# A recurrent attention with a feed-forward layer: negations ahead of masks, loads and stores moved among the queues, the A·B stage cut in halves

## The chip, the cores and the metric

The kernel runs on one core of a Trainium2 chip. A core has a matrix engine (TensorE, PE in the profile, with PEld for its weight loads), VectorE (DVE), ScalarE (ACT), GpSimd (POOL) and SyncE (SP), which here only issues DMAs. Each engine takes its instructions in the order of the program and waits on semaphores for the others; a DMA that waits on SP's queue holds up every DMA behind it. The metric is the device time of one execution in microseconds (us).

## The reference

Batch 4, 8 heads, 768 tokens, head size 40: 32 independent heads. Each keeps a 40x40 state that every token changes; the outputs go through a two-layer feed-forward net (called MoE in the code, though it has one expert).

```python
for t in range(S):
    y[:, :, t] = einsum('bhd,bhde->bhe', rt, state)
    Sa = einsum('bhde,bhe->bhd', state, at)
    state_decay = state * wt[:, :, None, :] - einsum('bhd,bhe->bhde', Sa, bt)
    state = state_decay + einsum('bhd,bhe->bhde', vt, kt)
...
h = x @ w_in                       # x: 3072 x 320, w_in: 320 x 2048
g = where(h >= 1, h, where(h <= -1, 0, (h + 1)**2 / 4))
return g @ w_out                   # w_out: 2048 x 320
```

All is float32.

## The kernel before, in words

**Chunks.** The 768 tokens are cut in 24 chunks of 32. Within a chunk the recurrence is written as matrix products, which need running products of w along the tokens and, for each head and chunk, the inverse of a triangular 32x32 matrix. Six sets of four chunks share this preparation; sets 0 and 1 are prepared before the main loop, but for the inverse of set 1.

**Three background stages** prepare a set s while the chunks of earlier sets run. *rows* (`prelude`, lines 217 to 262) takes four parts of eight tokens each. A part loads tiles of w, a, k and b (line 225), forms running products P of w on DVE (L237 to L243), multiplies a with them on POOL (L245), forms reciprocals on DVE (L249, L252), multiplies k (L255) and b (L257) with them on POOL, and stores the four products from the tile `arena` to a DRAM scratch `scr` (L258, issued by POOL). `arena` holds one part at a time. The tile of `b` is that of `a` (tag "a"). *ab* (`ab_set`, from line 276) reads rows of `scr` back into `tiab`, transposes them (L287, DVE), multiplies them in 32 small matmuls (L298), copies the result from PSUM (L303, ACT) and stores it to `abd` (L306). *inv* (`invert`) reads `abd` and inverts by 62 steps on POOL (L326 and L332) into `ttd`.

**The chain.** `chain(c, hb)` runs chunk c for heads 0 to 15 (hb 0) or 16 to 31 (hb 1) in five steps, with matmuls at L468, L479, L497, L526 and L536. After the second, DVE multiplies with the mask (L486) and ACT negates (L490); both read one of two PSUM tiles, of four head pairs each, and write one tile `cg`. At the fourth step ACT and POOL round the outputs into `Y` (L516, L517). `turn` (L423, L426, L428) transposes token rows from the tiles `ti`, `scores` multiplies them (L438) and masks them (L447). `cg` and `ti` are loaded from `scr` and `ttd` by L398, L401, L409 and L274.

**The feed-forward net.** After every second chunk `relayout` copies 64 tokens of `Y` into a tile `X` by nine DMAs on SP (L552 to L562). `moe` is a generator: for each of 16 blocks of 128 hidden columns, eight matmuls (L607), the activation on ACT (L613, L614) and DVE (L620), a split into a rounded part and a rest (L594 on ACT, L595 on POOL), and later six matmuls into `po` (L581, L585). At a group's end ACT copies `po` (L588) and SP stores it (L590).

**What sets the order.** The order is written out by hand. The main loop calls `step` ten times a chunk; a step runs one step of the chain, then three times `feed`, which takes 1024 columns of the feed-forward net's matmuls, and `background`. `feed` starts five steps after the first relayout, and from there one group of 64 tokens takes 20 steps, as long as two chunks. `background(n)` runs each stage in proportion to the weights that its generator yields, spread over a window of steps:

```python
WINDOWS = dict(
    rows=[(0, 0), (20, 36), (38, 68), (68, 103), (107, 147)],
    ab=[(0, 0), (38, 53), (68, 89), (108, 129), (147, 169)],
    inv=[(16, 36), (53, 72), (90, 112), (129, 152), (170, 192)],
)
ROWS_W = (2, 1, 1.5, 3, 2, 13)
AB_W = (1, 6, 3, 8, 15)
```

Steps within ten count unequally (`SHARE`). From step 192 on no background is left. Until the first relayout PE has only the chain, and `weights` converts the two weight matrices beside it.

## Time and profile before

| | us |
|---|---|
| median of 3 runs | 977.39 (974.42 to 980.83) |
| profiled execution | 976.18 |
| its span | 974.4 |
| PE busy | 775.0 (80%) |
| DVE busy | 590.4 (61%) |
| ACT busy | 478.6 (49%) |
| POOL busy | 443.8 (46%) |
| mean granted clock of TensorE | 0.85 |

In the profile, "L490" is line 490 of the kernel. A row of the order of time gives the start, the duration, the engine and line, what is written and read, the shape and the count of merged instructions, and in brackets how long the engine was idle before, and what ended that. "SPq" is a DMA issue on SyncE's queue. Names as "cg<-p" are tiles: written, then read.

### The profile page before, as it was taken

To read this page: it belongs to the slowest core of one execution; us is meant where nothing else is said; L and a number is where in the kernel's file an instruction comes from. 1 tells how busy PE (TensorE), PEld (TensorE's weight loads), DVE (VectorE), ACT (ScalarE), POOL (GpSimd) and SP (SyncE) were. 2 spreads that over 40 slices of the span, in tenths; PEclk is the share of its full clock that TensorE was granted. 3 is DMA by queue.
4 is the path that set the end of the run, shared out by engine and by line. 5 is a ranking of instruction groups with operands and counts; after the bars stand their busy time and mean duration, and the time that the engine had idled before them with its cause. 6 is when DMAs were issued, how large, how long until landed. Compare 5 with 4: busy or idle time off the path is not lost.

```text
span 974.4 us, 35827 instructions
## 1 busy us (share of the span) xinstructions
PE 775.0 (80%) x14976; PEld 692.1 (71%) x14976; DVE 590.4 (61%) x1562; ACT 478.6 (49%) x1230; POOL 443.8 (46%) x673
## 2 busy tenths in 40 slices
PE   4523543447886988799879798989999999999995
PEld 3312532336776887688879687978898899999995
DVE  7782876574756583775654774776665556655321
ACT  5822444212543544454445454546565566656663
POOL 5200223686331599332588232697235962222332
PEclk9755555575997789797999796999999999999998
DMA  8799995565677755896735886856855545552010
GB/s 274 148 193 245 202 207 151 141 139 134 146 156 152 163 138 115 178 186 130 179 100 117 182 160 133 173 135 131 146 115 121 110 101 111 105 90 56 16 36 14
DMA packets 276866, 134.64 MB, mean 138 GB/s; under 512 B 194984, under 2 KB 266856, under 8 KB 276704
## 3 DMA queue, kind: packets, MB, share of 16 engines
q1 hardware_dynamic: 273504, 121.20, 57.9%
q0 software_dynamic: 3200, 11.14, 3.8%
q8 instruction: 118, 1.93, 0.9%
q14 instruction: 44, 0.36, 0.1%
HBM read 96.83 MB, written 33.82 MB: 134 GB/s over the span
## 4 chain that ended last, share of the span: by engine, by line
PE 34%; DMA 16%; POOL 16%; DVE 12%; issue 8%; SPq 8%; ACT 4%; POOLq 0%; ACTq 0%; DVEq 0%
PE ph L607 11%; PE po L581 6%; POOL lw L326 5%; POOL lw L332 4%; DMA ti<-scr 4%; PE po L585 3%; PE p L497 3%; POOL gl L595 3%; SPq L274 3%; PE p L468 3%; PE p L526 2%; DMA ld_a<-in_a_dram 2%; PE p L438 2%; PE p L479 2%; PE p L536 1%
## 5 line engine op out<-in xcount | busy, mean ns | idle before, releaser
L607 PE MATMUL ph<-X,w 120*128 120x256 f32 x1536 | 260.9, 307 | 51.6 <-DVE qt L620 44.3
L595 POOL TENSOR_TENSOR gl<-qt,gh 128x256 fp32r<-128x256 f32 x192 | 140.9, 734 | 280.0 <-ACT gh L594 264.6
L607 PEld LDWEIGHTS ph<-X,w 120*128 120x128 f32 x1536 | 219.8, 203 | 68.1 <-DVE qt L620 51.3
L620 DVE SCALAR_TENSOR_TENSOR qt<-qt,ph 128x256 f32<-128x256 f32 x192 | 79.9, 416 | 150.3 <-ACT qt L614 148.3
L581 PE MATMUL po<-wide,gh 128*128 128x320 f32 x768 | 163.7, 329 | 0.3 <-ACT gh L594 0.3
L594 ACT CAST gh<-qt 128x256 fp32r<-128x256 f32 x192 | 78.0, 406 | 167.6 <-DVE qt L620 166.7
L581 PEld LDWEIGHTS po<-wide,gh 128*128 128x128 f32 x768 | 124.6, 202 | 3.7 <-ACT gh L594 0.5
L613 ACT ACTIVATE qt<-ph,half_c 128x256 f32<-128x256 f32 x192 | 91.1, 474 | 53.4 <-POOL gl L595 39.7
L585 PE MATMUL po<-wide,gl 128*128 128x320 f32 x384 | 99.6, 338 | 17.6 <-POOL gl L595 17.6
L497 PE MATMUL p<-cg 128*64 128x72 f32 (+1 forms) x1536 | 74.8, 262 | 44.2 <-DVE cg L486 39.7
L497 PEld LDWEIGHTS p<-cg 128*64 128x64 f32 x1536 | 66.8, 166 | 54.3 <-ACT cg L490 45.0
L326 POOL TENSOR_TENSOR lw<-lw 128x31 f32<-128x31 f32 (+15 forms) x155 | 94.4, 609 | 18.0 <-DMA lw<-abd 9.3
L490 ACT ACTIVATE cg<-p 32x160 f32<-32x160 f32 x192 | 56.8, 296 | 87.9 <-DVE cg L486 61.0
L447 DVE TENSOR_TENSOR cg<-p,mask 32x256 f32<-32x256 f32 x192 | 80.6, 420 | 25.8 <-PE p L438 23.2
L332 POOL TENSOR_TENSOR lw<-lw 128x31 f32<-128x31 f32 (+15 forms) x155 | 84.1, 543 | 8.8
L504 DVE SCALAR_TENSOR_TENSOR cg<-p,pr 40x160 f32<-40x160 f32 x184 | 59.1, 321 | 41.1 <-PE p L497 39.2
L614 ACT ACTIVATE qt<-qt 128x256 f32<-128x256 f32 x192 | 80.2, 418 | 6.1
L585 PEld LDWEIGHTS po<-wide,gl 128*128 128x128 f32 x384 | 65.6, 197 | 23.9 <-POOL gl L595 21.5
L468 PE MATMUL p<-cg 128*64 128x72 f32 x1536 | 66.4, 243 | 16.7 <-DMA cg<-ttd 15.0
L486 DVE SCALAR_TENSOR_TENSOR cg<-p,mask 32x128 f32<-32x128 f32 x192 | 55.2, 288 | 36.2 <-PE p L479 30.7
L468 PEld LDWEIGHTS p<-cg 128*64 128x64 f32 x1536 | 58.7, 149 | 23.6 <-issue 19.0
L526 PE MATMUL p<-ident,cg 40*64 40x40 f32 x1472 | 57.1, 238 | 1.9 <-issue 1.9
(104 smaller groups left out, 1027.9 us busy)
## 6 DMA issues: line engine op xcount, KB each, us to landing
ti<-scr SPq DMA_DIRECT2D x96, 200.0 KB
ti<-scr SPq DMA_DIRECT2D x96, 168.0 KB
scr<-arena POOLq DMA_DIRECT2D x16, 640.0 KB, 5.4
cg<-scr SPq DMA_DIRECT2D x96, 80.0 KB
X<-Y SPq DMA_DIRECT2D x36, 160.0 KB
scr<-wide SPq DMA_DIRECT2D x8, 640.0 KB
tiab<-scr SPq DMA_DIRECT2D x32, 160.0 KB
scr<-in_r_dram SPq DMA_DIRECT2D x24, 160.0 KB
```

Of the source, the lines that this page charges most:

```text
L326: eng.tensor_mul(t3, W3[:, 0:n, j : j + 1].broadcast_to([128, n, m]), L3[:, j + 1 :, j].unsqueeze(1).broadcast_to([128, n, m]),)
L332: eng.tensor_sub(W3[:, 0:n, j + 1 :], W3[:, 0:n, j + 1 :], t3)
L447: nc.vector.tensor_tensor(out=cg[q, f::2, C_X : C_X + 64][:, 4 * i : 4 * i + 4].rearrange("p h (j x) -> p h j x", x=32), in0=ps[quarter(f, ...
L468: nc.tensor.matmul(psv[h // 8][64 * (1 - f) : 64 * (1 - f) + 64, h // 2 % 4, 0:72], lhsT=cg[:, h, C_T : C_T + 64], rhs=cg[:, h, C_R : C_R ...
L497: nc.tensor.matmul(psv[h // 8][64 * f : 64 * f + 64, h // 2 % 4, 0:n3], lhsT=cgw[:, h * CW + C_G : h * CW + C_G + 64], rhs=cg[:, h, C_R : ...
L581: nc.tensor.matmul(pos[i], lhsT=gh[:, ts_], rhs=w2[f // 8][:, j, f % 8, :], start=f == 0 and j == 0, stop=False)
L585: nc.tensor.matmul(pos[i], lhsT=gl[:, ts_], rhs=w2[f // 8][:, 0, f % 8, :], start=False, stop=f == NF - 1)
L595: nc.gpsimd.tensor_sub(gl, gt, gh.bitcast(F32))
L607: nc.tensor.matmul(ph, lhsT=w1[:, wi, fs], rhs=Xs[g][:, xi, :], start=i == 0, stop=i == 7)
L613: nc.scalar.activation(gt, ph, AF.Relu, bias=half_c, scale=0.5)
L614: nc.scalar.activation(gt, gt, AF.Square)
L620: nc.vector.scalar_tensor_tensor(out=gt, in0=gt, scalar=1.0, in1=ph, op0=ALU.min, op1=ALU.max)
```

## The change

- `ab_set` works on halves of eight head pairs: two transposes, 16 matmuls and one ACT copy of 128x128 each, in place of four, 32 and one of 128x256. The tile `ea` is half as large. Its weights `AB_W` are new. The early code that used the whole tile takes a second tag.
- `prelude` gives b a tile of its own. The first part's four loads go together. After that, the next part's a is asked for once the reciprocals are listed, w after the product with k, and k and b after the store.
- In `chain` the four negations on ACT are listed ahead of the four masks on DVE, both in the order half 0, half 1.
- ACT issues the output store.
- The two token loads (`load_ti`) and the relayout, but for the first and the last group, go one step later in the main loop.

```diff
--- before.py
+++ after.py
@@ -33,7 +33,7 @@
 SHARE = (3.1, 1.45, 0.93, 2.03, 0.6) * 2
 
 ROWS_W = (2, 1, 1.5, 3, 2, 13)
-AB_W = (1, 6, 3, 8, 15)
+AB_W = (1, 4, 8, 3, 6, 30)
 INV_W = 12
 
 TRAIL = 5
@@ -137,8 +137,6 @@
     turned = [
         [x[:, 0:2048].rearrange("p (n t) -> p n t", t=L) for x in xs] for xs in ((cgf[0], cgf[1]), (cgf[2], Yraw))
     ]
-
-    early_rows = {}
 
     def early_load(s):
         for x, n in zip(early_in[s], "wabk"):
@@ -190,9 +188,8 @@
     def early_ab(s, half):
 
         ps = psum()
-        if half == 0:
-            early_rows[s] = work.tile([128, 16, 2, 32], F32, tag="ea", name="ea").rearrange("p a b x -> p (a b x)")
-        ab = early_rows[s][:, 512 * half : 512 * half + 512]
+        tag = "ev" if half else "ea"
+        ab = work.tile([128, 8, 2, 32], F32, tag=tag, name=tag).rearrange("p a b x -> p (a b x)")
         for c in (2 * half, 2 * half + 1):
             for h in range(NH):
                 p, f = h // 2, h % 2
@@ -225,7 +222,7 @@
             nc.sync.dma_start(t, srcs[n][:, 4 * s : 4 * s + 4, 8 * part : 8 * part + 8, :])
             return t
 
-        wl, al, kl = load("w", 0, "w"), load("a", 0, "a"), load("k", 0, "k")
+        wl, al, kl, bl = (load(n, 0, n) for n in "wakb")
         pad_scr(s)
         yield 10
         for part in range(4):
@@ -244,21 +241,25 @@
             yield ROWS_W[0]
             nc.gpsimd.tensor_mul(at[:, 1:], al[:, 1:], P[:, :7])
             yield ROWS_W[1]
-            bl = load("b", part, "a")
             rec = work.tile([128, 8, D], F32, tag="ld_rec", name="rec")
             nc.vector.reciprocal(rec[:, 7], P[:, 7])
             yield 0.6
             for t in range(7, 0, -1):
                 nc.vector.tensor_mul(rec[:, t - 1], rec[:, t], wl[:, t])
                 yield 0.4
+            more = part < 3
+            if more:
+                al = load("a", part + 1, "a")
             yield ROWS_W[2]
             nc.gpsimd.tensor_mul(kt, kl, rec)
+            if more:
+                wl = load("w", part + 1, "w")
             yield ROWS_W[3]
             nc.gpsimd.tensor_mul(bt, bl, rec)
             nc.gpsimd.dma_start(scr[s][0 : NH * 128, 80:240].rearrange("(p t) x -> p t x", t=L)[:, ts_, :], R)
             yield ROWS_W[4]
-            if part < 3:
-                wl, al, kl = load("w", part + 1, "w"), load("a", part + 1, "a"), load("k", part + 1, "k")
+            if more:
+                kl, bl = load("k", part + 1, "k"), load("b", part + 1, "b")
             yield ROWS_W[5]
 
     def load_rows(dst, c, off, n, h0=0, nh=NH):
@@ -279,34 +280,38 @@
             reclaim(9)
             pad_rows(tiab, 48)
         load_rows(tiab, 4 * s, O_A, 80)
-        yield AB_W[4]
+        yield AB_W[5]
+        tv = tiab.rearrange("p h (j x) -> p h j x", x=40)[:, :, :, 0:32]
         for c in range(4 * s, 4 * s + 4):
-            ea = work.tile([128, 16, 2, 32], F32, tag="ea", name="ea")
-            tv = tiab.rearrange("p h (j x) -> p h j x", x=40)[:, :, :, 0:32]
-            for i in range(4):
-                nc.vector.transpose(ea[:, 4 * i : 4 * i + 4], tv[:, 4 * i : 4 * i + 4])
-                yield AB_W[0]
-            if c < 4 * s + 3:
-                load_rows(tiab, c + 1, O_A, 80)
-            yield AB_W[1]
-            ps = psum()
-            for p in range(16):
-                for f in range(2):
-                    rows = slice(64 * f, 64 * f + D)
-                    q = 2 * f + p % 2
-                    sl = p // 2
-                    nc.tensor.matmul(
-                        ps[32 * q : 32 * q + 32, 32 * sl : 32 * sl + 32],
-                        lhsT=ea[rows, p, 0, :], rhs=ea[rows, p, 1, :], start=True, stop=True,
-                    )
-            ab = work.tile([128, 8, 32], F32, tag="ab", name="ab")
-            nc.scalar.copy(ab, ps[:, 0:256].rearrange("p (s x) -> p s x", x=32))
-            yield AB_W[2]
+            for half in range(2):
+                if half:
+                    yield AB_W[2]
+                ea = work.tile([128, 8, 2, 32], F32, tag="ea", name="ea")
+                for i in range(2):
+                    nc.vector.transpose(ea[:, 4 * i : 4 * i + 4], tv[:, 8 * half + 4 * i : 8 * half + 4 * i + 4])
+                    yield AB_W[0]
+                if half and c < 4 * s + 3:
+                    load_rows(tiab, c + 1, O_A, 80)
+                yield AB_W[1]
+                if half == 0:
+                    ab = work.tile([128, 8, 32], F32, tag="ab", name="ab")
+                ps = psum()[:, 0:128]
+                for p in range(8):
+                    for f in range(2):
+                        rows = slice(64 * f, 64 * f + D)
+                        q = 2 * f + p % 2
+                        sl = p // 2
+                        nc.tensor.matmul(
+                            ps[32 * q : 32 * q + 32, 32 * sl : 32 * sl + 32],
+                            lhsT=ea[rows, p, 0, :], rhs=ea[rows, p, 1, :], start=True, stop=True,
+                        )
+                nc.scalar.copy(ab[:, 4 * half : 4 * half + 4], ps.rearrange("p (s x) -> p s x", x=32))
+            yield AB_W[3]
             for q in range(4):
                 nc.sync.dma_start(
                     abd[c // 4][q // 2, c % 4, q % 2 :: 2].rearrange("h t i -> t h i"), ab[32 * q : 32 * q + 32]
                 )
-            yield AB_W[3]
+            yield AB_W[4]
 
     def invert(s):
 
@@ -348,7 +353,7 @@
             done[key] = s
             yield 0
 
-    done, size, spent = dict(rows=1, ab=1), dict(rows=10 + 4 * (6.2 + sum(ROWS_W)), ab=AB_W[4] + 4 * (4 * AB_W[0] + sum(AB_W[1:4])), inv=INV_W + 67), {}
+    done, size, spent = dict(rows=1, ab=1), dict(rows=10 + 4 * (6.2 + sum(ROWS_W)), ab=AB_W[5] + 4 * (4 * AB_W[0] + 2 * AB_W[1] + sum(AB_W[2:5])), inv=INV_W + 67), {}
     back = {k: staged(*a) for k, a in dict(
         rows=("rows", None, prelude), ab=("ab", "rows", ab_set), inv=("inv", "ab", invert)).items()}
 
@@ -482,12 +487,13 @@
                 )
         for i in range(2):
             for f in range(2):
-                q = uq[f]
+                nc.scalar.mul(cg[uq[f], f::2, C_S : C_S + D][:, halves[i]], psv[i][quarter(f, i), :, 32:72], -1.0)
+        for i in range(2):
+            for f in range(2):
                 nc.vector.scalar_tensor_tensor(
-                    out=cg[q, f::2, C_R : C_R + 32][:, halves[i]], in0=psv[i][quarter(f, i), :, 0:32], scalar=-1.0,
+                    out=cg[uq[f], f::2, C_R : C_R + 32][:, halves[i]], in0=psv[i][quarter(f, i), :, 0:32], scalar=-1.0,
                     in1=mask[quarter(f, i)].unsqueeze(1).broadcast_to([32, 4, 32]), op0=ALU.mult, op1=ALU.mult,
                 )
-                nc.scalar.mul(cg[q, f::2, C_S : C_S + D][:, halves[1 - i]], psv[1 - i][quarter(f, 1 - i), :, 32:72], -1.0)
         yield
         psv = psum_2()
         n3 = 32 if last else 72
@@ -587,7 +593,7 @@
                     ob = mp.tile([128, 320], F32, tag="ob", name="ob", bufs=2)
                     nc.scalar.copy(ob, pos[i])
                     m = 128 // nt
-                    nc.sync.dma_start(ov[m * i : m * i + m, t0 : t0 + nt, :], ob)
+                    nc.scalar.dma_start(ov[m * i : m * i + m, t0 : t0 + nt, :], ob)
                 yield 320
 
         def split(g, f, gt, gh, gl):
@@ -844,6 +850,14 @@
             background(now[0] + (k + 1) / 3)
         now[0] += 1
 
+    def relayout_due(c):
+        g = c // 2 - 1
+        if c % 2 == 0 and g >= 0:
+            reclaim(5 + g % 2)
+            Xs[g] = relayout(g)
+            if idle[0]:
+                owed[0], idle[0] = -TRAIL * 3072, False
+
     for c in range(NC + 1):
         nxt = c + 1 < NC
         if c < NC:
@@ -851,18 +865,19 @@
         if nxt:
             load_cg(c + 1, 0)
         step(c, 0)
+        if 0 < c < NC - 1:
+            load_ti(c + 1, 1)
         if 0 < c < NC:
             scores(c, 1)
         step(c - 1, 1)
-        for g, (t0, nt) in enumerate(groups):
-            if t0 + nt == 32 * c:
-                reclaim(5 + g % 2)
-                Xs[g] = relayout(g)
-                if idle[0]:
-                    owed[0], idle[0] = -TRAIL * 3072, False
+        moved = idle[0] or c == NC
+        if moved:
+            relayout_due(c)
         if nxt:
             turn(c + 1, 0, 0)
         step(c, 0)
+        if not moved:
+            relayout_due(c)
         if nxt:
             turn(c + 1, 0, 1)
         step(c - 1, 1)
@@ -871,12 +886,12 @@
         step(c, 0)
         if nxt:
             turn(c + 1, 0, 2)
-            if c + 2 < NC:
-                load_ti(c + 2, 0)
         gens[c, 1] = chain(c, 1)
         if nxt:
             load_cg(c + 1, 1)
         step(c, 1)
+        if c + 2 < NC:
+            load_ti(c + 2, 0)
         if nxt:
             scores(c + 1, 0)
         step(c, 0)
@@ -889,8 +904,6 @@
         step(c, 1)
         if nxt:
             turn(c + 1, 1, 2)
-            if c + 2 < NC:
-                load_ti(c + 2, 1)
     for _ in mgen:
         pass
 
```

## The prediction

> **What bounds the kernel now.** I read the page first (shares, the clock row, the chain of waits), then the sums by stretch, then who waited for whom, and last the order of time around the longest waits. The page:
>
> ```profile
> span 974.4 us, 35827 instructions
> PEclk9755555575997789797999796999999999999998
> PE 34%; DMA 16%; POOL 16%; DVE 12%; issue 8%; SPq 8%; ACT 4%; POOLq 0%; ACTq 0%; DVEq 0%
> ```
>
> The profiled execution took 976.18 us, 1.8 more than its span; the median of the runs shown, 977.39, is 1.2 above that. TensorE (PE) holds a third of the chain of waits; DMA, GpSimd (POOL), VectorE (DVE) and SyncE's queue hold half. The sums by stretch show where; I cut them where the chain of heads 0 to 15 begins chunks 2, 4, 9, 13, 19 and 23 (a chunk is ten steps; chunks 9 to 12 are left out, and the last row is a short piece that I use below). Columns: stretch, its length, busy time of each engine, granted clock, DMA share, GB/s.
>
> ```profile
> 161.60:261.30 99.70, 59.26 (x1046) 53.03 (x1045) 63.72 (x170) 31.27 (x82) 63.40 (x98) 0.70 0.56 130
> 261.30:459.70 198.40, 173.18 (x3315) 153.36 (x3314) 124.33 (x369) 88.09 (x237) 94.37 (x141) 0.84 0.74 155
> 606.10:787.20 181.10, 173.52 (x3617) 155.47 (x3616) 115.79 (x305) 102.25 (x272) 114.78 (x184) 0.98 0.62 128
> 787.20:897.20 110.00, 110.00 (x2241) 99.93 (x2240) 67.57 (x180) 68.68 (x183) 34.12 (x53) 1.00 0.48 98
> 444.70:449.80 5.10, 5.10 (x107) 4.18 (x107) 0.01 (x1) 1.86 (x6) 0.73 (x1) 0.50 0.49 120
> ```
>
> From 787.2, with no background work left, four chunks take 110.0 us, 2.75 a step, and PE is busy throughout: nothing here touches that. From 261.3 to 459.7 five chunks take 198.4, 3.97 a step, 61 more than at 2.75; PE idles 25 of it, and most of the rest is a clock of 0.84. So what is to be won lies between 161.6 and the start of chunk 13, where the row products (rows) and the A·B matrices (ab) are made beside the chain. Who waited there (us in total, times, longest):
>
> ```profile
> ACT cg L490 <- DVE cg L486: 61.0, 20, 11.0
> DVE arena L239 <- DMA ld_a<-in_a_dram: 24.9, 5, 12.1
> POOL arena L257 <- DMA ld_b<-in_b_dram: 18.4, 7, 6.9
> DVE ea L287 <- DMA tiab<-scr: 18.4, 6, 6.0
> SPq L274 <- DVE pr L428: 63.1, 16, 10.4
> SPq L590 <- ACT ob L588: 41.8, 4, 27.2
> PE ph L607 <- DMA X<-Y: 6.5, 7, 2.2
> ```
>
> DVE is in order: while it waits for a load, the chain's masks (L486) and the MoE's L620 stand behind it, then ScalarE (ACT) behind L486, then PE behind L620.
>
> **Rows' loads.** The load of `a` for the next part used to need the tile that `b` had, so it could leave only after L257, the last product. Now it needs L245 only; `w` needs the reciprocals. Four waits hold 24.4 of the 24.9 us. But L239 writes the arena, which POOL's store L258 must have read: that wait comes next. The rows of the four, and the four stores before them:
>
> ```profile
> 188.35 0.96 POOL L258 DMA_DIRECT2D scr<-arena  x1 [0.30 <-POOL arena L257]
> 196.77 0.20 DVE L239 TENSOR_TENSOR arena<-ld_a,arena 128x40 f32<-128x40 f32 x1 [5.30 <-DMA ld_a<-in_a_dram]
> 236.01 0.93 POOL L258 DMA_DIRECT2D scr<-arena  x1 [0.30 <-POOL arena L257]
> 242.26 0.20 DVE L239 TENSOR_TENSOR arena<-ld_a,arena 128x40 f32<-128x40 f32 x1 [12.06 <-DMA ld_a<-in_a_dram]
> 409.94 0.93 POOL L258 DMA_DIRECT2D scr<-arena  x1 [0.30 <-POOL arena L257]
> 419.80 0.20 DVE L239 TENSOR_TENSOR arena<-ld_a,arena 128x40 f32<-128x40 f32 x1 [1.89 <-DMA ld_a<-in_a_dram]
> 435.30 0.93 POOL L258 DMA_DIRECT2D scr<-arena  x1 [0.30 <-POOL arena L257]
> 449.80 0.20 DVE L239 TENSOR_TENSOR arena<-ld_a,arena 128x40 f32<-128x40 f32 x1 [5.13 <-DMA ld_a<-in_a_dram]
> DMA to landing us min/median/max: 4.6/5.4/7.1
> ```
>
> With the median 5.4 the stores land at 193.8, 241.4, 415.3 and 440.7. DVE can start that much earlier: 3.0, 0.9, 1.9 (all of its wait) and 5.1 (all), 10.9 us together. PE does not get all of it: ahead of 449.80 it was busy 5.10 of 5.10. I take two thirds, **-7**; ends 0 and -11.
>
> `b` now has a tile of its own and is asked for with `k`, a part earlier than it is used, so the 18.4 us of L257 go, most of them in two waits:
>
> ```profile
> 315.53 0.87 POOL L257 TENSOR_TENSOR arena<-ld_b,rec 128x320 f32<-128x320 f32 x1 [6.15 <-DMA ld_b<-in_b_dram]
> 468.36 0.86 POOL L257 TENSOR_TENSOR arena<-ld_b,rec 128x320 f32<-128x320 f32 x1 [6.89 <-DMA ld_b<-in_b_dram]
> 471.26 0.90 PE L585 MATMUL po<-wide,gl 128*128 128x320 f32 x2 [2.29 <-POOL gl L595]
> ```
>
> After the second, PE lost 2.29 us on the MoE's gl queued behind it on POOL, a third of the 6.89. A third of 18.4 would be 6; the small waits cost nothing that I see, so **-4**; ends 0 and -6. The fourth load at a set's start goes last of the four and delays no first operand: 0; ends 0 and +1.
>
> **SyncE's queue.** The 24 output stores leave SP for ACT, and with them waits of 41.8 us for the copy, of which most lie after 897, where little is queued behind:
>
> ```profile
> SPq L590 <- ACT ob L588: 32.4, 2, 27.2
> ```
>
> The token loads go one step later, behind the six loads of the cg tile and no longer ahead of them; the relayout goes behind the third step's row loads. All arrive in time: token rows keep six steps (16.5 us at 2.75). The relayout's nine issues:
>
> ```profile
> 876.08 2.38 SPq L552 DMA_DIRECT2D X<-Y  x3
> 878.50 2.96 SPq L558 DMA_DIRECT2D X<-Y  x4
> 881.50 1.46 SPq L562 DMA_DIRECT2D X<-Y  x2
> 885.80 0.64 PE L607 MATMUL ph<-X,w 120*128 120x256 f32 x4
> ```
>
> They take 6.9 us on SP, and the MoE's first use is 9.7 us after the first. SP stood idle ahead of 876.08, waiting for POOL to round Y, so where no background runs a step's delay in the list moves nothing: 0; ends 0 and +2.75 for each of nine groups, +25. What SP's freedom is worth shows at one place of before, where a tiab load stood behind such a relayout:
>
> ```profile
> 278.91 1.06 DVE L287 STREAM_TRANSPOSE ea<-tiab 128x256 f32<-128x256 f32 x3
> 284.87 2.01 SPq L562 DMA_DIRECT2D X<-Y  x2
> 286.99 2.01 SPq L274 DMA_DIRECT2D tiab<-scr  x4
> 293.09 1.42 DVE L287 STREAM_TRANSPOSE ea<-tiab 128x256 f32<-128x256 f32 x4 [6.00 <-DMA tiab<-scr]
> 297.46 0.80 PE L607 MATMUL ph<-X,w 120*128 120x256 f32 x2 [4.37 <-DVE qt L620]
> ```
>
> DVE waited 6.00 and PE lost 4.37 after it. One such loss is what I credit SP with: **-4**; ends 0 and -10. Storing from ACT costs ACT an issue of its own, 24 x about 0.6 (a DMA issue above takes 0.5 to 0.8) = 14; ACT was busy 68.68 of 110.00 at the tightest, so **+1**; ends 0 and +14. The Trainium skill, page "DMA: Bandwidth & Descriptors", section "Issuing engines are not separate DMA queues", says that issuing from a second engine saves only the issuing time; by that rule the move gives the 14 us of issue to SP and no faster transfer.
>
> **The ab stage.** It is cut in halves of eight head pairs: transposes and matmuls stay in number, ACT's 16 copies become 32 half as wide (+16 x some 0.3, hidden as above). The weights matter more. Before, a set weighed 15 + 4 x 21 = 99, and from a tiab load to its transposes lay 6 + 3 + 8 = 17; now 30 + 4 x 29 = 146 and 4 + 3 + 6 = 13. Over windows of 15, 21, 21 and 22 steps that was 2.6, 3.6, 3.6 and 3.8 steps; it becomes 1.3, 1.9, 1.9 and 2.0: at 3.97 a step (3.02 in the last, 181.1 over 60 steps) 5.3, 7.4, 7.4 and 6.0 us. The load itself took 293.09 - 286.99 = 6.1 from its first issue. If SP is 2 us late (it was 7.0 late above; the new places lie mostly clear of the relayout and of the cg loads) the three such loads of a set wait 2.8, 0.7, 0.7 and 2.1 each, 19 us in all against 18.4 now. The planner's shares are uneven, down to one step, so I add 6 us of DVE waiting, at the 4.37 of 6.00 seen: **+4**; ends -6 and +35. The abd stores before the next copy lose time alike; inside these ends.
>
> **Negations first.** ACT's L490 shares each PSUM half with DVE's L486. Before, ACT began in the other half and then waited for DVE (61.0 us). Now ACT goes first and no longer stands behind a stalled DVE; instead each mask follows its negation.
>
> ```profile
> 862.94 1.29 DVE L486 SCALAR_TENSOR_TENSOR cg<-p,mask 32x128 f32<-32x128 f32 x4 [0.60 <-PE p L479]
> 863.00 1.23 ACT L490 ACTIVATE cg<-p 32x160 f32<-32x160 f32 x4 [0.58 <-PE p L479]
> 867.04 1.22 PE L497 MATMUL p<-cg 128*64 128x72 f32 x32
> ```
>
> Side by side they took 1.3 us; in file, 1.23 + 0.32. The next matmuls come 2.8 us after, so the 0.3 is covered by the other chain's step; uncovered it would be 48 x 0.3 = 15. In a stall, ACT saves its two late negations, 0.6 x 20 = 12 at most. Net **-2**; ends -12 and +15. The Trainium skill, page "PSUM — Partial Sum Buffer", section "Terms", has it that two engines may not touch one bank and quadrant at once, reads included; by that rule the masks must follow in file at every stage, which speaks against this order and would cost the 15 if nothing covered it.
>
> **The sum.** -7 - 4 - 4 + 1 + 4 - 2 = -12. Idling also lowers the clock: in the 5.10 us quoted at 0.50, PE was busy and did half the work, 2.6 us lost. I credit two such stretches, **-5**; ends 0 and -20. So 976.2 - 17 = 959; on the median, **960 us**.
>
> **The rivals.** *Waits replaced (no change).* Behind `a` stands the store's landing, behind `b` POOL's own inversion, behind SP's waits its issues, and the clock stays: only a's first 3.0 and half of what I credit `b`, SP and ACT with (5) remain, 8 less the 4 and 1 that ab and ACT's issues cost: 974, range 967 to 983. For it: two of the four waits end within 3.0 us of the landing. Chance 0.27.
> *The tiab loads become the bound (slower).* If SP stays as late as at 286.99, 7.0 us, each load needs 13.1, and the twelve wait 7.8, 5.7, 5.7 and 7.1 each: 79 us, 60 more than now; at 4.37 of 6.00 that is +44, for the +4 in the sum: 1000. With the other gains kept, it makes the kernel slower than before from a lateness of about 4.4 us, and by 1% from 5.5. Against it: the relayout and token loads, which made SP late, have moved. Chance 0.16.
> *The clock comes back (faster still).* In 261.3 to 459.7 PE was busy 173.2 at 0.84, 28 us of clock; in 161.6 to 261.3, 59.3 at 0.70, 18. If PE's stalls fall short enough, half of that 46 returns: 960 + 5 - 23 = 942. [...] Chance 0.12.
>
> **How the numbers follow.** The forecast has 0.45 (950 to 969). This kernel's runs tell 1% apart, 9.8 us: under 967.6 is faster, over 987.2 slower. Faster: 0.43 of the forecast, 0.12 of the clock, 0.02 of the replaced waits: 0.57; slower 0.16; within 1% 0.27. The range 940 to 983 leaves out most of the slower rival, 0.15, and 0.05 below.
>
> **What would show it.** Right: no wait of L239 on ld_a over 2 us but for landings of the arena's store; none of L257 on ld_b; ACT no longer waiting for L486; the clock above 0.84 from 261 to 460. Wrong: DVE's waits on tiab well over 18.4 us, PE's on X<-Y over 6.5, or DVE's masks waiting for ACT for tens of us with PE idle behind them; or the steps after the background's end longer than 2.75.

## The result, and the profile after

The changed kernel takes **1019.67 us** (1016.38 to 1022.89), the kernel before beside it 975.9: a ratio of **1.0439, 95% interval 1.0384 to 1.0494**. The forecast of 960 us and its range of 940 to 983 were wrong, and so was the sign. Of a few kernels below, one execution was over 1.5% longer than the fastest; the ratios leave such executions out, the medians do not.

The page of the changed kernel: span, clock by slices, shares of the chain of waits, and one of the DMA queues.

```profile
span 1019.6 us, 35949 instructions
PEclk9655555577776798886999887979798999999998
PE 37%; DMA 15%; POOL 13%; DVE 13%; issue 8%; SPq 7%; ACT 4%; DVEq 0%; POOLq 0%; ACTq 0%
q10 hardware_dynamic: 3120, 3.93, 1.2%
```

The shares hardly differ from before: the page alone doesn't say where 45 us went. q10 is new: the 24 output stores, 3.93 MB together, that ACT issues. The mean clock fell from 0.85 to 0.824.

The sums by stretch say where. These are cut at the beginnings of the same chunks as the rows before (2, 4, 9, then 13, 19, 23).

```profile
172.90:273.60 100.70, 65.16 (x1045) 57.74 (x1045) 65.02 (x170) 31.70 (x82) 63.33 (x98) 0.66 0.59 139
273.60:485.60 212.00, 179.05 (x3313) 157.94 (x3312) 125.40 (x366) 90.10 (x245) 93.36 (x140) 0.81 0.65 141
634.10:829.60 195.50, 185.70 (x3617) 166.10 (x3616) 118.33 (x314) 103.98 (x278) 116.17 (x185) 0.91 0.57 120
829.60:941.50 111.90, 110.59 (x2243) 100.02 (x2242) 66.45 (x176) 69.25 (x182) 34.20 (x53) 1.00 0.44 96
```

Up to chunk 2 the changed kernel loses 11.3 us (172.9 against 161.6), in the next two chunks 1.0 (100.7 against 99.7), in chunks 4 to 8 **13.6** (212.0 against 198.4, clock 0.81 against 0.84), in 9 to 12 2.1 (148.5, 485.6 to 634.1, against 146.4, 459.7 to 606.1), in 13 to 18 **14.4** (195.5 against 181.1, clock 0.91 against 0.98), in the four chunks without background 1.9, and in the tail 0.9. That sums to 45.2, the difference of the spans. Three places hold nearly all: the start, and two stretches where *rows* and *ab* run.

Who waited there (waits of the changed kernel: us in total, times, longest):

```profile
DVE cg L493 <- ACT cg L490: 52.6, 30, 4.2
DVE ea L291 <- DMA tiab<-scr: 50.8, 11, 9.8
ACT ab L308 <- DMA abd<-ab: 23.5, 5, 9.0
DVE ev L431 <- DMA abd<-ev: 14.4, 1, 14.4
DVE arena L236 <- DMA ld_a<-in_a_dram: 11.1, 1, 11.1
```

L493 is the mask, which was L486; L291 the transposes of ab, which were L287. The waits for the rows' loads went as forecast: none on `ld_b` is left, and one of five on `ld_a`. What came in their place is larger: the transposes wait 50.8 us for `tiab` in place of 18.4, the copies of ab 23.5 for the stores of the copy before, and the masks 52.6 for ACT, in the place of ACT's 61.0 for the masks. The fourth line is a wait that the prediction does not have at all.

The waits of SP's queue in the changed kernel (L222 is `load`, L275 `load_rows`, L311 the stores of ab, L403 and L406 the loads of cg):

```profile
SPq L311 <- DMA out_dram<-ob: 25.1, 5, 7.5
SPq L275 <- DMA out_dram<-ob: 23.4, 3, 10.0
SPq L222 <- DMA out_dram<-ob: 11.2, 2, 8.2
SPq L406 <- DMA out_dram<-ob: 7.2, 2, 3.6
SPq L403 <- DMA out_dram<-ob: 6.8, 2, 3.4
```

73.7 us in these five rows: SP, which no longer issues the output stores, waits for them. None of the waiting DMAs reads or writes `out` or `ob`. One of them, in order of time (SP, then ACT from the same stretch), and below it three pieces of the chain of waits at the same place (start, duration, what):

```profile
692.19 2.23 SPq L275 DMA_DIRECT2D tiab<-scr  x3
...
698.36 0.52 ACTq L596 DMA_DIRECT2D out_dram<-ob  x1
...
699.38 0.52 ACTq L596 DMA_DIRECT2D out_dram<-ob  x1
...
704.41 0.30 SPq L275 DMA_DIRECT2D tiab<-scr  x1
```

```profile
693.08 4.08 DMA tiab<-scr
698.36 6.03 DMA out_dram<-ob
704.41 4.05 DMA tiab<-scr
```

Three of a `tiab` load's four DMAs go out from 692.19. The fourth leaves at 704.41, ten microseconds after the third: it stood for the store that ACT issued only at 698.36, and then for that store's landing, 6.03 us later. The trace gives the semaphore that each DMA signals. SP's use eight, ACT's 24 stores the same eight, and POOL's eight others. The store of 698.36 and the fourth load signal the same one, number 108, and the fourth load's instruction waits on it before it goes. So the reading is: a DMA of SP that takes a semaphore whose last user was a store of ACT waits until that store has landed; the store itself waits for `po`, at the group's end; so SP is held by the end of the feed-forward group. The Trainium skill, page "DMA: Bandwidth & Descriptors", section "Why a DMA increments its semaphore by 16 and not by 1", says that a wait can pass too early where two DMAs in flight share one semaphore, which would be a reason for this order; the row above agrees in that the later DMA did not leave before the earlier one had landed, 6.03 us after its issue at 698.36.

### The profile page after: what moved, and what is told of

The parts are those of the page before. It is cut to its first block, busy times and chain, and to the rows that moved or that the text cites. A ratio compares the mean times of both kernels' runs of the same rounds, so it can differ in the third digit from the quotient of the medians.

```text
span 1019.6 us, 35949 instructions
## 1 busy us (share of the span) xinstructions
PE 800.5 (79%) x14976; PEld 712.8 (70%) x14976; DVE 594.1 (58%) x1562; ACT 483.3 (47%) x1246; POOL 443.2 (43%) x673
## 3 DMA queue, kind: packets, MB, share of 16 engines
q10 hardware_dynamic: 3120, 3.93, 1.2%
## 4 chain that ended last, share of the span: by engine, by line
PE 37%; DMA 15%; POOL 13%; DVE 13%; issue 8%; SPq 7%; ACT 4%; DVEq 0%; POOLq 0%; ACTq 0%
PE ph L613 12%; PE po L587 6%; POOL lw L331 4%; POOL lw L337 4%; PE po L591 4%; DMA tiab<-scr 3%; PE p L532 3%; PE p L503 3%; PE p L473 2%; POOL gl L601 2%; PE p L443 2%; DVE arena L240 2%; PE p L484 2%; PE p L542 2%; SPq L275 2%
## 5 line engine op out<-in xcount | busy, mean ns | idle before, releaser
L613 PE MATMUL ph<-X,w 120*128 120x256 f32 x1536 | 272.8, 315 | 46.0 <-DVE qt L626 41.5
L613 PEld LDWEIGHTS ph<-X,w 120*128 120x128 f32 x1536 | 228.3, 210 | 64.4 <-DVE qt L626 49.9
L587 PE MATMUL po<-wide,gh 128*128 128x320 f32 x768 | 167.1, 334 | 0.4 <-ACT gh L600 0.4
L587 PEld LDWEIGHTS po<-wide,gh 128*128 128x128 f32 x768 | 127.4, 206 | 3.8 <-ACT gh L600 0.7
L503 PE MATMUL p<-cg 128*64 128x72 f32 (+1 forms) x1536 | 71.5, 254 | 37.0 <-DVE cg L493 37.0
L452 DVE TENSOR_TENSOR cg<-p,mask 32x256 f32<-32x256 f32 x192 | 80.6, 420 | 27.9 <-PE p L443 25.3
L503 PEld LDWEIGHTS p<-cg 128*64 128x64 f32 x1536 | 63.8, 160 | 47.1 <-DVE cg L493 37.8
L493 DVE SCALAR_TENSOR_TENSOR cg<-p,mask 32x128 f32<-32x128 f32 x192 | 55.3, 288 | 56.2 <-ACT cg L490 52.6
L473 PEld LDWEIGHTS p<-cg 128*64 128x64 f32 x1536 | 58.9, 149 | 23.5 <-issue 14.8
L478 ACT COPY x<-p 128x288 f32<-128x288 f32 x96 | 36.6, 398 | 53.3 <-PE p L473 50.0
```

Of the source, the lines that this page charges most:

```text
L452: nc.vector.tensor_tensor(out=cg[q, f::2, C_X : C_X + 64][:, 4 * i : 4 * i + 4].rearrange("p h (j x) -> p h j x", x=32), in0=ps[quarter(f, ...
L473: nc.tensor.matmul(psv[h // 8][64 * (1 - f) : 64 * (1 - f) + 64, h // 2 % 4, 0:72], lhsT=cg[:, h, C_T : C_T + 64], rhs=cg[:, h, C_R : C_R ...
L503: nc.tensor.matmul(psv[h // 8][64 * f : 64 * f + 64, h // 2 % 4, 0:n3], lhsT=cgw[:, h * CW + C_G : h * CW + C_G + 64], rhs=cg[:, h, C_R : ...
L587: nc.tensor.matmul(pos[i], lhsT=gh[:, ts_], rhs=w2[f // 8][:, j, f % 8, :], start=f == 0 and j == 0, stop=False)
L613: nc.tensor.matmul(ph, lhsT=w1[:, wi, fs], rhs=Xs[g][:, xi, :], start=i == 0, stop=i == 7)
```

## The experiments

Times are medians, ratios are to the kernel before on the same chip, with 95% intervals. "After" is the changed kernel.

### Undoing one part of the change

**The store back on SP** (sp_store).

```diff
-                    nc.scalar.dma_start(ov[m * i : m * i + m, t0 : t0 + nt, :], ob)
+                    nc.sync.dma_start(ov[m * i : m * i + m, t0 : t0 + nt, :], ob)
```

> The changed kernel, with the 24 output stores issued by SyncE again. Theory A (a semaphore shared across queues): in the changed kernel 74 us of SyncE's waits are put down to DMA out_dram<-ob (25.1, 23.4, 11.2, 7.2 and 6.8), because a load or store on SyncE that takes the semaphore last used by a store of ScalarE's must wait until that store was issued, at a group's end, and has landed. Then those waits go, the four tiab loads no longer take 12.5 us to issue as at 692.2, and the time falls from 1019.7 by 10 to 20, to 1000 to 1010. Theory B (the shorter gap between a tiab load and its transposes is what costs): the stores are innocent, and the time stays within 3 us of 1019.7.

Measured: 1011.57 us, ratio 1.0341 (1.0254 to 1.0429); after had 1.0439 (1.0384 to 1.0494), and the intervals overlap. SP's waits for the landings are gone, except at the program's end, but SP now waits itself, since the store stands in its list right behind the copy:

```profile
SPq L596 <- ACT gh L600: 56.7, 9, 9.8
SPq L596 <- ACT ob L594: 32.4, 2, 27.2
```

In before, the second of them was 41.8, and the first less than half (SP's queue in before):

```profile
SPq L590 <- ACT gh L594: 24.6, 6, 9.1
```

So in the changed kernel SP stands for the stores on either queue, and undoing the move alone did not show what it is worth.

**The early code's second half in another tile** (early_x0). The early code makes two halves for each of two sets. Their tile `ev` carries the same tag as the tile of `turn` (L431), so `turn` for chunk 0 waits for the early halves' stores to land. Here the second half uses `x0`, a tile of another stage.

```diff
-        tag = "ev" if half else "ea"
-        ab = work.tile([128, 8, 2, 32], F32, tag=tag, name=tag).rearrange("p a b x -> p (a b x)")
+        if half:
+            ab = work.tile([128, 8, 72], F32, tag="x0", name="x0").rearrange("p a x -> p (a x)")[:, 0:512]
+        else:
+            ab = work.tile([128, 8, 2, 32], F32, tag="ea", name="ea").rearrange("p a b x -> p (a b x)")
```

> The changed kernel, with the second half of each early A-B matrix in the tile x0, which is first used later, in place of ev. In the changed kernel VectorE waits 14.4 us at 53 to 68 us for the store of that half before it may transpose token rows into ev, and chunk 0 begins 11.9 us later than before (91.5 against 79.6). If that wait is the cause, it goes and the time falls by 9 to 12, to 1008 to 1011. If the next wait (the inverse of set 0, the scr stores on SyncE) comes at the same moment, it falls by under 3.

Measured: 1006.94, ratio 1.0332 (1.0289 to 1.0375). Chunk 0 begins at 79.4 in place of 91.5, as in before (79.6). The first line is of the changed kernel, in the order of time:

```profile
68.04 0.71 DVE L431 STREAM_TRANSPOSE ev<-ti 128x512 f32<-128x512 f32 x1 [14.44 <-DMA abd<-ev]
```

and in early_x0 the same transpose follows L430 with no wait:

```profile
53.11 0.71 DVE L433 STREAM_TRANSPOSE ev<-ti 128x512 f32<-128x512 f32 x1
```

DVE's 14.4 us at the start are paid by the kernel nearly in full: 12.1 us of it.

**Wider spacing of ab** (ab_gaps). After, with weights by which a `tiab` load has 13 + 3 + 4 = 20 of 135 to its transposes, near before's 17 of 99, in place of 13 of 146.

```diff
-AB_W = (1, 4, 8, 3, 6, 30)
+AB_W = (1, 4, 2, 3, 13, 15)
```

> The changed kernel, with the weights of the ab stage set so that a tiab load has 20 of 135 units (15%) before its transposes, near the 17 of 99 of before, in place of 13 of 146 (9%). Theory B: VectorE's waits on tiab fall from 50.8 us (11 times) to 18 to 25, and the time by 12 to 22, to 998 to 1008. Theory A: the loads are late because SyncE is held, the waits stay above 35, and the time falls by under 5.

Measured: 1013.18, ratio 1.0394 (1.0341 to 1.0446), within the interval of after. The wait went, the time did not:

```profile
DVE ea L291 <- DMA tiab<-scr: 25.0, 6, 9.9
```

26 us less of DVE waiting, and some 4 of the kernel (0.0045 of 976), which the intervals do not tell from none. A theory that put the loss on the spacing alone falls here.

**All three together** (three_undone): the edits of sp_store, early_x0 and ab_gaps in one kernel.

```diff
-AB_W = (1, 4, 8, 3, 6, 30)
+AB_W = (1, 4, 2, 3, 13, 15)
...
-        tag = "ev" if half else "ea"
...
-                    nc.scalar.dma_start(ov[m * i : m * i + m, t0 : t0 + nt, :], ob)
+                    nc.sync.dma_start(ov[m * i : m * i + m, t0 : t0 + nt, :], ob)
```

> The changed kernel with the output stores on SyncE, the second half of the early A-B matrix in x0, and the ab weights with 15% between a tiab load and its transposes. Left of the change: rows' loads, ab in halves, negations first, token loads and relayout later. If the three are the whole loss and what is left has the worth that I predicted (-7 -4 for the loads, -2 for the negations), the time is 960 to 972. If the losses of the three only add up from their single runs (8, 13 and 6 us off 1019.7), it is about 992, and 16 us of loss lie in what is left.

Measured: 985.61, ratio 1.0072 (1.0032 to 1.0112). One at a time the three took 0.010, 0.011 and 0.004 off the ratio, 0.025 in sum; together 0.037, 36 us of the 43. So these three hold most of the loss. That together they gain more than in sum would fit causes that hide one another, but the difference of 0.012 is within the intervals of the five ratios.

### One part alone in the kernel before

**The store by ACT** (act_store_only).

```diff
-                    nc.sync.dma_start(ov[m * i : m * i + m, t0 : t0 + nt, :], ob)
+                    nc.scalar.dma_start(ov[m * i : m * i + m, t0 : t0 + nt, :], ob)
```

> The kernel before, with the 24 output stores issued by ScalarE and nothing else changed. Theory A: SyncE's waits on out_dram<-ob rise from some 13 us to over 50, and the kernel gets 8 to 15 us slower than before, about 987. My prediction's price (ScalarE's issues, +1, SyncE freed, -4): 974, within 4 us of before. Theory B says nothing of it and expects no change.

Measured: 1019.5, ratio **1.0468** (1.0412 to 1.0524): one line costs as much as the whole change. SP's waits, and the pieces of the chain of waits that are an output store's flight:

```profile
SPq L274 <- DMA out_dram<-ob: 47.7, 8, 9.5
SPq L409 <- DMA out_dram<-ob: 30.2, 4, 10.2
SPq L225 <- DMA out_dram<-ob: 13.6, 3, 8.0
```

```profile
304.14 7.51 DMA out_dram<-ob
543.71 8.01 DMA out_dram<-ob
623.92 8.88 DMA out_dram<-ob
702.06 8.03 DMA out_dram<-ob
```

The waits sum to 91.5 us, and four stores that nobody reads stand on the chain that ends last, 32.4 us of it.

**The store by POOL** (pool_store_only). If the shared semaphores are the cause, an engine whose DMAs signal others should not have this cost, though it too stands for the copy.

```diff
-                    nc.sync.dma_start(ov[m * i : m * i + m, t0 : t0 + nt, :], ob)
+                    nc.gpsimd.dma_start(ov[m * i : m * i + m, t0 : t0 + nt, :], ob)
```

> The kernel before, with the 24 output stores issued by GpSimd in place of SyncE and nothing else changed. GpSimd's DMAs have eight semaphores of their own in the trace, ScalarE's took them from the eight of SyncE's. Theory A (SyncE waits for the landing of a store whose semaphore it shares): SyncE no longer waits for out_dram<-ob, and the time is within 12 us of before (966 to 990, the upper end if GpSimd's own wait for the copy holds its queue), far below the 1019.5 of the store on ScalarE. Its rival (a store that is not on SyncE lands late or loads the DMA engines badly, whatever the semaphores): 1005 to 1025 again.

Measured: 985.45, ratio 1.0083 (1.0041 to 1.0126). Of SP's waits on `out_dram` only the last one of the program is left (L922, which waits for all output), and POOL stands little:

```profile
SPq L922 <- DMA out_dram<-ob: 42.5, 1, 42.5
```

```profile
POOL out_dram L590 <- ACT ob L588: 10.6, 8, 1.4
```

That is the theory's case: the same stores, off SP, on semaphores that SP does not use, cost 0.8% and not 4.7%. Its rival, that a store off SP lands late or loads the DMA engines badly whatever its semaphore, asked for 1005 us or more.

**Negations first** (neg_first_only).

```diff
+                nc.scalar.mul(cg[uq[f], f::2, C_S : C_S + D][:, halves[i]], psv[i][quarter(f, i), :, 32:72], -1.0)
+        for i in range(2):
+            for f in range(2):
                 nc.vector.scalar_tensor_tensor(
...
-                nc.scalar.mul(cg[q, f::2, C_S : C_S + D][:, halves[1 - i]], psv[1 - i][quarter(f, 1 - i), :, 32:72], -1.0)
```

> The kernel before, with the negations ahead of the masks and nothing else changed. As predicted (-2): 974, ScalarE no longer waiting for L486, the masks behind the negations hidden. The rival: in the changed kernel VectorE waited 52.6 us in 30 cases for L490, up to 4.2 us, because ScalarE comes to the negations late; then the kernel loses 5 to 15, 981 to 991.

Measured: 982.27, ratio 1.007 (1.0039 to 1.0101), +7 us. The waits changed sides, 52.1 us of DVE's for ACT in place of 61.0 of ACT's for DVE:

```profile
DVE cg L488 <- ACT cg L485: 52.1, 30, 6.5
```

By the starts of their chains, chunks 20 and 22, where no background runs, take 28.1 us in place of 27.4; chunk 21 takes 27.5 in both. The two profiled executions differ by 5.3 us, and 4.7 of them lie from chunk 19 on (1.8 in chunks 19 to 22, 2.9 after the start of chunk 23), though only 14.5 of the 52.1 us of waits do. In these two executions the other 37.6 us of waits, where the background runs, thus went with a loss of 0.6.

**Token loads and relayout later** (late_only).

```diff
+        if 0 < c < NC - 1:
+            load_ti(c + 1, 1)
...
+        if not moved:
+            relayout_due(c)
...
-            if c + 2 < NC:
-                load_ti(c + 2, 0)
...
+        if c + 2 < NC:
+            load_ti(c + 2, 0)
...
-            if c + 2 < NC:
-                load_ti(c + 2, 1)
```

> The kernel before, with the token loads and the relayout a step later and nothing else changed. As predicted (the -4 of SyncE's freedom): 972, within 4 us of before. The rival: the relayout's lateness costs the MoE; in the changed kernel chunks 20 and 22, with no background, take 28.1 us in place of 27.4, 0.7 for each group, so +5 to +8 in all, 981 to 984.

Measured: 969.83, ratio **0.9914** (0.9877 to 0.9951), -8 us: the one part of the change that gains. In the profiled execution chunks 0 to 8 are 9.5 us shorter than in before, and the rest is 3.2 longer. DVE's waits for `tiab` are 12.2 us in place of 18.4:

```profile
DVE ea L287 <- DMA tiab<-scr: 12.2, 6, 4.6
```

That this wait is the cause is not shown: in late_store, below, it is 27.9 us, and the kernel is faster still. SP's waits for the stores' data are hardly less than before (35.3 us for L594 and 32.0 for L588, against 24.6 and 41.8), so this is not the freedom of SP that the prediction credited to the stores.

**ab in halves with the change's weights** (ab_only); the early second half is in `x0`, so that the start isn't disturbed.

```diff
-AB_W = (1, 6, 3, 8, 15)
+AB_W = (1, 4, 8, 3, 6, 30)
...
+            for half in range(2):
+                if half:
+                    yield AB_W[2]
+                ea = work.tile([128, 8, 2, 32], F32, tag="ea", name="ea")
...
```

> The kernel before, with the ab stage in halves and its new weights (the second half of the early matrices in x0), nothing else changed. Theory B: VectorE's waits on tiab rise from 18.4 to about 50 us and the time by 15 to 25, to 991 to 1001. Theory A (only the store on ScalarE makes the tiab loads late): the waits stay under 30, and the time within 5 us of before.

Measured: 1031.57, ratio **1.0576** (1.0509 to 1.0642), +56 us. From the groups by line (busy, mean ns | idle before it and what ended that):

```profile
L291 DVE STREAM_TRANSPOSE ea<-tiab 128x256 f32<-128x256 f32 x64 | 25.3, 425 | 59.9 <-DMA tiab<-scr 53.1 <-DMA abd<-ab 6.5 <-PE p L304 0.3
L308 ACT COPY ab<-p 128x128 f32<-128x128 f32 x32 | 8.4, 262 | 33.5 <-DMA abd<-ab 20.2 <-PE p L304 12.4 <-PE p L443 0.7
```

The group of the copies in before:

```profile
L303 ACT COPY ab<-p 128x256 f32<-128x256 f32 x16 | 5.9, 367 | 11.1 <-DMA abd<-ab 5.6 <-PE p L497 2.5 <-DMA cg<-scr 1.1
```

DVE's wait for `tiab` is 34.7 us longer than before (18.4), and ACT's for `abd<-ab` 14.6.

**The same halves with the wider spacing** (ab_even_gaps).

```diff
-AB_W = (1, 4, 8, 3, 6, 30)
+AB_W = (1, 4, 2, 3, 13, 15)
```

> The kernel before with the ab stage in halves as in the change, but with 15% of the set's weight between a tiab load and its transposes (9% in the change), the rest as before. If the weights are what costs, VectorE's waits on tiab fall from 53.1 us to 25 or less and the time from 1031.6 to within 10 us of before, 977 to 987. If the halves cost by themselves (32 copies and two waits of a set's chunk for PE in place of one, a smaller ea that holds back the transposes), it stays above 1005.

Measured: 987.97, ratio 1.0129 (1.0039 to 1.0219). Of the +56 us the weights are some 44, and the halves themselves some 13 (4 to 21 by the interval). DVE's wait for `tiab` is 20.7, before's size again. The wait that stays larger is that of the copies (5.6 in before), which also wait 15.1 us for their matmuls (1.1 or less in before); that these waits are what the halves cost is not shown:

```profile
ACT ab L308 <- DMA abd<-ab: 19.8, 3, 10.2
```

**A short spacing without halves** (short_gap_only): before's whole tiles, with 9 of 100 weights from load to transposes.

```diff
-AB_W = (1, 6, 3, 8, 15)
+AB_W = (1, 3, 2, 4, 48)
```

> The kernel before, ab in whole tiles as before, with weights that leave 9% of a set's window between a tiab load and its transposes (17% before, 9% in the change). If the share is the cause, VectorE's waits on tiab rise from 18.4 to 40 us or more and the time to 1000 to 1025. If it takes the halves as well, the waits stay under 30 and the time under 988.

Measured: 1007.89, ratio 1.0233 (1.0142 to 1.0324), by the same wait:

```profile
DVE ea L287 <- DMA tiab<-scr: 54.6, 9, 13.0
```

So a shorter way from load to use costs with and without the halves. Nearly the same waiting for `tiab` (54.6 and 53.1 us) goes with a loss of 23 here and of 56 in ab_only, so the sum of one wait is no price. The 13 us of the halves themselves make up part of the difference; the rest is open.

**Rows' loads** (rows_only, and rows_late with the later token loads). The room for a tile of `b` came here from keeping one output tile `ob` in place of two.

```diff
-        wl, al, kl = load("w", 0, "w"), load("a", 0, "a"), load("k", 0, "k")
+        wl, al, kl, bl = (load(n, 0, n) for n in "wakb")
...
-            bl = load("b", part, "a")
...
+            if more:
+                al = load("a", part + 1, "a")
...
-                    ob = mp.tile([128, 320], F32, tag="ob", name="ob", bufs=2)
+                    ob = mp.tile([128, 320], F32, tag="ob", name="ob", bufs=1)
```

> The kernel before, with the rows' loads each asked for once their operand is used up and a tile of its own for b (the room comes from a single output tile ob in place of two), nothing else changed. As predicted (-7 for a and w, -4 for b, and the clock): 958 to 968, with VectorE's waits on ld_a under 14 us and GpSimd's on ld_b under 3. The rival (the store of the arena lands last anyway, and PE had other work): the waits go and the time stays within 4 us of before, 973 to 981.

> The kernel before, with the rows' loads as in the change (one ob tile) and the token loads and relayout a step later; ab, masks and output store as before. The later loads alone gave 0.9% less. If the two gains add up: 8 us less than with the rows' loads alone, 950 to 962. If both only free the same waits on SyncE, no more than the better of the two alone, about 966.

Measured: 1038.48, ratio 1.0634 (1.0542 to 1.0726), and 1032.23, ratio 1.0544 (1.0468 to 1.0621). Neither says anything of the loads, because ACT's second copy now waits for the first one's store (the row of rows_only):

```profile
ACT ob L592 <- DMA out_dram<-ob: 81.2, 12, 10.6
```

**One output tile alone** (one_ob_only) tests that.

```diff
-                    ob = mp.tile([128, 320], F32, tag="ob", name="ob", bufs=2)
+                    ob = mp.tile([128, 320], F32, tag="ob", name="ob", bufs=1)
```

> The kernel before with one output tile ob in place of two, nothing else changed. If the single tile is what cost in the run of the rows' loads alone (1038.5), ScalarE waits some 80 us for out_dram<-ob here too and the time is 1020 to 1045. If it is the loads, the time stays within 10 us of before.

Measured: 1040.49, ratio 1.059 (1.0521 to 1.0658), with the same wait:

```profile
ACT ob L588 <- DMA out_dram<-ob: 80.5, 12, 11.1
```

Within the intervals, the tile explains both runs whole.

### Without the side effects

**Rows' loads on the halves** (rows_halves): ab_even_gaps, plus the edit of rows_only with two `ob`. **And with the later loads** (rows_halves_late), which is three_undone without the negations.

```diff
-        wl, al, kl = load("w", 0, "w"), load("a", 0, "a"), load("k", 0, "k")
+        wl, al, kl, bl = (load(n, 0, n) for n in "wakb")
...
+        if not moved:
+            relayout_due(c)
```

> The kernel before with ab in halves at 15% (as ab_even_gaps, 988.0) and the rows' loads as in the change, two ob tiles. As predicted for the loads (-11, with the clock -16): 972 to 977. If the store of the arena and POOL's own work come next and PE had other work: the waits on ld_a and ld_b go and the time stays within 4 us of 988.

> As rows_halves, with the token loads and relayout a step later as well; this is the run with three parts undone (985.6) without the negations first. If the negations cost the 7 us that they cost alone, 978 to 980; if they cost nothing here, 985.6 within 4.

Measured: 987.53, ratio 1.0062 (1.0029 to 1.0095), and 979.28, ratio 0.9997 (0.9961 to 1.0033). The first has the median of ab_even_gaps (987.97); by the ratios it is 0.0067 lower, within the intervals. The rows' loads are thus worth at most a few us and nothing that these runs tell from none, although their waits went: none on `ld_b`, and on `ld_a` (in rows_halves)

```profile
DVE arena L240 <- DMA ld_a<-in_a_dram: 11.1, 1, 11.1
DVE arena L240 <- DMA scr<-arena: 5.4, 2, 3.2
```

The second line stood at one wait of 1.7 us in before: DVE now waits for the landing of POOL's store instead. The later loads gain 0.0065 here, near the 0.0086 alone. And three_undone, which has the negations beside it, is 0.0075 above, as neg_first_only had it.

### A version that beats both

**The store a little later on SP** (late_store): late_only, and the output store stays on SP but is listed two steps after the copy, to spare SP the wait for it.

```diff
-                    nc.sync.dma_start(ov[m * i : m * i + m, t0 : t0 + nt, :], ob)
+                    stores.append([now[0] + 2, lambda a=ov[m * i : m * i + m, t0 : t0 + nt, :], x=ob: nc.sync.dma_start(a, x)])
...
         now[0] += 1
+        while stores and stores[0][0] <= now[0]:
+            stores.pop(0)[1]()
```

> The kernel before with the token loads and relayout a step later (969.8 alone), and the output stores still on SyncE but listed two steps after their copies. If SyncE's waits for the copies (35.3 us on gh L594, 32.0 on ob L588 of which 27 lie in the tail) hold back loads that others need, they go and the time falls by 4 to 10, to 960 to 966. If nothing urgent stood behind them, it stays within 3 us of 969.8.

> As rows_halves_late (979.3), with the output stores on SyncE listed two steps later. If the store's place costs what late_store shows, it falls by the same; if the ab stage in halves is what holds it, it stays above 975.

Measured: 960.52 (956.32 to 966.35), ratio **0.9806** (0.9756 to 0.9857). The before beside it has a median of 982.11 from 17 executions, somewhat high; against before's 977.39 it is 0.983. The interval lies below that of late_only, so the later store gains about 1% more. The same on top of rows_halves_late (late_store_rows) gave 973.76, ratio 0.9936 (0.9898 to 0.9974): 0.0061 off (the intervals overlap), and 0.013 above late_store, which is what the halves cost in ab_even_gaps. How the later store gains is not shown: of SP's waits at the stores, 67.3 us in late_only (35.3 for ACT's casts, 32.0 for its copies), 58.6 are still there (26.3 and 32.3), so two steps are not always enough:

```profile
SPq L590 <- ACT gh L594: 26.3, 4, 9.1
```

## Why the prediction was wrong

Each term of the sum beside what the runs showed (a ratio less 1, of 976 us):

| term | predicted | measured |
|---|---|---|
| rows' loads, a and w | -7 | with b's tile: 0 (by ratios -7, not told from 0) |
| b's own tile | -4 | |
| SP freed (the later loads and relayout themselves: 0) | -4 | later loads and relayout alone: -8 |
| store issued by ACT | +1 | **+46** alone |
| ab stage | +4 | **+56** alone |
| negations first | -2 | +7 |
| early tag `ev` | not seen | +12 by the start of chunk 0 (+10 by ratios) |
| clock | -5 | 0.85 to 0.824, a loss |

**The store on ACT is the step that failed**: "The 24 output stores leave SP for ACT, and with them waits of 41.8 us for the copy". The waits did not leave with the stores: in the changed kernel SP stood 73.7 us for their landings. I priced the issue (24 at 0.52 measured, 0.6 assumed) and gave ends of 0 and +14; the queue that loses the stores I only credited. Yet before had no DMA from ACT, so nothing in it bounded what ACT's DMAs do to SP's, and an end of the range worked out from ACT's issues alone was not a bound. act_store_only shows the loss, 46 us in place of the +1 and of the -4; the shared semaphores and pool_store_only show its cause.

**The ab stage is the second step that failed, and it was the slower rival, which I held to be the least likely but one.** "The tiab loads become the bound" had the mechanism: three short windows, loads in SP's queue, DVE behind them. I took SP 2 us late and got 19 + 6 us of waiting; ab_only shows 53.1 + 6.5, the size of a lateness between 4 and 5 (the 12 loads wait 19 at 2 and 79 at 7.0, so 12 us more for each us later, and 6 come on top). What spoke against it, that relayout and token loads had moved, was worth 6 us of `tiab` waits in late_only. Its price, 4.37 of 6.00, did not fail by itself: in short_gap_only 36 us more of waiting went with a loss of 23, which is below that price. In ab_only 41 us more (53.1 + 6.5 less 18.4) would be 30 by it, and the loss is 56; the halves themselves, whose copies the prediction took for hidden, bring some 13 of the rest. The waits of the copies for the abd stores, put "inside these ends", are 14.6 us more of ACT, and ab_even_gaps still has them.

**The early tag** stands in the diff, and I did not follow who else has the tag `ev`. Its price could have been foreseen in kind: four stores at the start, with the next user of that tile on the way to chunk 0.

**Rows' loads**: the waits went as drawn, to the row (one of 11.1 is left, where 0.9 of 12.06 was to be gained), and the time did not follow. Here the first rival fits: the landing of the arena's store comes next (5.4 us in rows_halves, 1.7 in before). Two thirds of a waiting DVE was too much where PE "was busy 5.10 of 5.10" ahead of one of them.

**SP freed, and the later loads and relayout.** These moves stood at 0 by themselves and gain 8; that the sign is that of the -4 is luck. The -4 was read at one place, a `tiab` load behind a relayout with 6.00 us of waiting. In late_only that load still stands behind that relayout (the relayout from 273.58, the load at 282.01, DVE's wait 3.57), PE now waits 3.51 for the relayout there in place of 4.37 for DVE's result, and SP's waits for the stores are as in before. The code moves ten relayouts later, not nine; only an end of the range hung on it.

**Negations**: the bounds held, the sign did not. The credit was for ACT's stalls, and the runs put the stall on DVE instead (52.1 us against 61.0), with DVE the busier of the two. The step that failed is the cover: the next matmuls 2.8 us later were to hide the 0.32 us. Chunks 20 and 22 pay 0.7 each, which is two stages at 0.32 with nothing covered, and chunk 21 pays none; why they differ is open. The Trainium skill, page "PSUM — Partial Sum Buffer", section "Terms", says that two engines may not touch one bank and quadrant at once, reads included. The 30 waits of L488 for ACT, 52.1 us, agree that the masks stood behind the negations.

**Clock**: the mechanism may stand, as idling went up and the clock down (0.81 for 0.84, 0.91 for 0.98 in the two stretches); the forecast of less idling fell. Which idling lowers the clock, the 5.10 us at 0.50 did not show: PE's last idle ahead of them was 1.39 us long and ended at 441.52.

**What stays open.** The parts sum to 46 + 56 + 12 + 7 - 8 + 0 = 113 us (the 12 from undoing the tag in the changed kernel, the 0 of the rows' loads on the halves, the others alone in before), the whole change costs 43. So parts of it hide one another, but how is not shown: no run has just the store and ab. That both hold up the same `tiab` loads would fit the row at 704.41 and ab_gaps (26 us of waits less, 4 us of time); against it, the store alone raised DVE's waits for `tiab` only from 18.4 to 23.8 us in act_store_only and cost 46. Nor is it shown which wait takes the rows' gain, or by which wait the later loads and the later store gain.

## What to carry to other kernels

Here a DMA that moved to another queue left a wait behind, because the queue that it left shared its completion semaphores. Before such a move, find out from the trace which semaphores each queue's DMAs signal, and where a queue stands for a store's data, first try to list the store later on that queue (about 1% here). Do not price a change by the sum of one wait: 54 us of it went with 23 us in one kernel and 56 in another. When a planner's weights are retuned, work out the time from each load to its use in every window, and set it against the load's flight with the queue as late as it was at its worst. A tile tag reused "early" is a dependency: follow each tag to its next user.

## What the runs showed that I had not expected

- DMAs issued by ACT and by SP signalled the same eight semaphores, and SP's later DMAs waited for ACT's to land: 91.5 us of SP's time in act_store_only, with a store's landing as long as 8.88 us on the chain. POOL's signalled others, and SP waited for no store of POOL's before the program's end.
- A single output tile in place of two cost 5.9%, with 12 waits of up to 11.1 us for a store of 128x320 to land, in a kernel that stores 24 such tiles.
- A 0.9% gain came from only listing loads and the relayout a step later, with not one instruction removed.
